# A routed expert network on one core: the first token list from 96 columns, the rest of the second list in a third piece, logits in groups of 24 matmuls, six search rounds

## The chip, the cores and the metric

The kernel runs on 1 core of one Trainium2 chip. The metric is the device time in microseconds (us) of one execution; several executions are made and the median is taken. The engines are TensorE (PE, its weight loads PEld), VectorE (DVE), ScalarE (ACT), GpSimd (POOL) and SyncE (SP), which here only issues DMA transfers.

## The reference

```python
# x (8, 3584, 192), weight (8 heads, 7 taps): a causal 7-tap filter, softmax weights per head
w = softmax(weight, axis=-1)
out = einsum('hk,bskhg->bshg', w, windows_of_7(x))      # -> 28672 tokens x 192
# routing: every (token, expert) pair in order of falling logit; a token goes to its first
# expert that still has room (3584 tokens each)
logits = out @ w_gate                                    # 28672 x 8
for idx in argsort(-logits.flatten()):
    tok, e = idx // 8, idx % 8
    if assigned[tok] < 0 and counts[e] < 3584: assigned[tok] = e; counts[e] += 1
# expert networks: h = relu(x @ w1[e]) (192 x 1024), y = h @ w2[e] (1024 x 192)
```

## The kernel before, in words

**Filter stage.** 16 half batches of 1792 tokens. `conv` (line 196) makes 8 PE matmuls per half batch, one per head (tile `cv`), ACT copies each to tile `a`, and the result is stored to `attn` in DRAM. DVE transposes `a` in four steps to `aT` (`transp`, 208); PE multiplies it with the gate matrix in six calls of four matmuls (`logits`, 217, tile `pl`; three `gate` steps of 8 matmuls each); `end` transposes the logits (tile `pt`) into `LT`, 16 columns per half batch, 256 in all, and takes each token's best logit (`top`).

**Routing in the background.** `Route` is a chain of generators whose steps `Steps.hook` (95) slips between the filter's and then the experts' instructions. A clock model (`Meter`, `Pace`) estimates when PE, DVE and ACT reach a point; a step is emitted only when its inputs should be there by that model. All engines run in program order, so a step emitted too early makes its engine wait. `thresh` finds a threshold `Ts`: tokens whose best logit is above it can be placed at once. From them two lists are made, each from 128 columns: `settle` marks them (`F`), `count` counts them with 8 matmuls, `place` computes each token's slot (18 matmuls with a base), `slots` prepares the operands, `sort` makes slot order with 128 one-hot matmuls (`oa`, eight per DVE instruction), `turn` transposes with 16 matmuls, `gather` adds up the list with 17 matmuls and `tokens` turns it into indices (`ia` where to write, `ja` where to read). The second list uses `sort4`, whose result goes through DRAM: two stores to `otab`, eight loads back (tile `X`, lines 546 and 563, all on SP); `gather` is emitted 10 us (`TURN`) after its last ACT copy by the model. `open` and `rounds` (743) then search the remaining tokens' thresholds in seven rounds (`ROUNDS`, 249), `final` marks the last tokens, and a last pair of lists (columns 128 to 255, then 0 to 127) is made with `sort4`.

**Experts.** 56 tiles of 512 tokens; tiles 0 to 7 come from the first list, 8 to 31 from the second, 32 to 55 from the last pair. Per tile 40 matmuls `ph` (`l1`, 1301) and 64 matmuls `y` of the tile before (`l2`, 1320), in eight steps f = 0 to 7. Rows are fetched two tiles ahead by four indirect DMAs on POOL (`gather`, 1268). Tiles 8 to 31 are transposed by DVE and a trip through DRAM (`scr`, lines 1396 to 1399, on SP); tile 0 by PE (`bg<-ident,xg`, `evac` to `xa` and `xd`). While tiles 0 to 7 run, the weights of the eight experts are loaded (`raw`), split into high and low parts (`wsplit`, 1219) and kept in DRAM (`kw`, `kv`), from which later tiles load them.

**Joints.** `half(0)`, `tail`, `half(1)` and `rest` run in this order (line 1535). `first` (1565) fetches tiles 0 and 1 as soon as `half(0)` is done (`got`). From half batch `LAG` = 13 on, the queue `left` of transposes and logit steps stands still until `got`, then two of its steps follow each `conv` matmul (`mid`, 1603). `idx_of` (1641) drains what is left of the second list before tile 8's rows are fetched (in tile 6), and of the last lists before tile 32's (in tile 30).

Of the kernel before, what the change touches and what calls it, by code (L numbers as in the profile page):

```python
# [248 lines left out]
ROUNDS = [(8, 1.0, False, 16)] + [(16, 1.0, False, 8)] * 2 + [(16, 0.5, True, 8)] * 2 + [(0, 0.0, True, 8)] * 2  # L249
# [10 lines left out]
class Route:  # L260
# [15 lines left out]
    def consts(self):  # L276
# [12 lines left out]
        self.g1 = cst.tile([128, 2], F32, name="g1")  # L289
        for h in range(2):  # L290
            P.tensor_scalar(self.g1[:, h:h + 1], pf, 1.0 + 128 * h, None, op0=OP.add)
# [81 lines left out]
    def settle(self, h):  # L373

        V, wk = self.nc.vector, self.wk
        s = slice(128 * h, 128 * h + 128)
        yield "cols", 128 * h + 128
        if h == 0:
            self.F = wk.tile([128, 8, G], BF, name="F")
        m = wk.tile([128, 128], F32, name="m_f")  # L380
        V.scalar_tensor_tensor(m, self.M1[:, s], self.Ts, self.M1[:, s], op0=OP.is_lt, op1=OP.add)
        for q in range(2):
            e = slice(4 * q, 4 * q + 4)
            V.tensor_tensor(self.F[:, e, s], self.LT[:, e, s], m[:, None, :].to_broadcast([128, 4, 128]),
                            op=OP.is_equal)
            yield PEW if q else None


    def count(self, F, h):
        nc, wk = self.nc, self.wk  # L390
        V, PE = nc.vector, nc.tensor
        s = slice(128 * h, 128 * h + 128)
        if h == 0:
            self.tot = [None, None]
            self.sl = wk.tile([128, G], F32, name="sl")
        ps = self.bg()
        for e in range(8):
            PE.matmul(ps[:, e:e + 1], F[:, e, s], self.ones[:, 0:1], start=True, stop=True, skip_group_check=True)
        t = self.tot[h] = wk.tile([128, 8], BF, name="tot%d" % h)
        nc.scalar.activation(t, ps[:, 0:8], AF.Copy)  # L400
        yield PEA

    def place(self, F, h, base):
# [3 lines left out]
        s = slice(128 * h, 128 * h + 128)  # L407
        SP = wk.tile([128, 8, 128], F32, name="X0")
        for q in range(2):
            ps = self.bg()  # L410
            f = F[:, 4 * q:4 * q + 4, s]
            PE.matmul(ps, self.U, f, start=True, stop=False, skip_group_check=True)
            for u in range(4):
                e = 4 * q + u
                o = ps[:, 128 * u:128 * u + 128]
                b = lambda t: t[:, e:e + 1].to_broadcast([128, 128])
# [3 lines left out]
            V.scalar_tensor_tensor(SP[:, 4 * q:4 * q + 4], ps.rearrange("p (e g) -> p e g", g=128), 1.0, f,  # L420
                                   op0=OP.add, op1=OP.mult)
            yield
        for u in range(2):
            z = slice(64 * u, 64 * u + 64)
# [3 lines left out]
    def columns(self, h, nt, base):  # L428
# [3 lines left out]
        ps = self.bg()  # L432
        PE.matmul(ps[:, 0:8], self.U, self.tot[h], start=True, stop=base is None)
        if base is not None:
            PE.matmul(ps[:, 0:8], self.ones, self.tot[base], start=False, stop=True)
        bi = wk.tile([128, 2, 8], I32, name="c_bi")
# [4 lines left out]
        c = wk.tile([128, 2, 8], F32, name="c_f")  # L441
        V.tensor_scalar(c[:, 0], bi[:, 0], 2.0, None, op0=OP.mult)
        V.tensor_scalar(c[:, 1], bi[:, 1], 2.0, 1.0, op0=OP.mult, op1=OP.add)
        oh = self.oh = wk.tile([128, 2, 8, 2, 16], BF, name="c_oh")
        V.tensor_tensor(oh[:, :, :, 0, 0:nt].rearrange("p w e t -> p (w e) t"),
                        self.iq[:, None, 0:nt].to_broadcast([128, 16, nt]),
                        c.rearrange("p w e -> p (w e)")[:, :, None].to_broadcast([128, 16, nt]), op=OP.is_equal)
        V.tensor_scalar(oh[:, :, :, 1, 0:nt].rearrange("p w e t -> p (w e) t"),
                        oh[:, :, :, 0, 0:nt].rearrange("p w e t -> p (w e) t"), self.g1[:, h:h + 1], None, op0=OP.mult)

    def slots(self, F, h, first):
# [4 lines left out]
        s = slice(128 * h, 128 * h + 128)  # L456
        si = wk.tile([128, 128], I32, name="m_i")
        qi = wk.tile([128, 128], I32, name="m_j")
# [3 lines left out]
        if first:  # L462
            V.tensor_copy(self.q, qi)
# [4 lines left out]
        for w in range(2):  # L468
            pw = wk.tile([128, 128], BF, name="pw")
            V.tensor_scalar(pw, si, 128.0 * w, self.p1, op0=OP.is_equal, op1=OP.mult)  # L470
            yield
            V.tensor_tensor(b[:, w], F[:, :, s], pw[:, None, :].to_broadcast([128, 8, 128]), op=OP.mult)
        yield

    def sort(self, h, nt, base, per=8):

        nc, wk = self.nc, self.wk
        V, A, PE = nc.vector, nc.scalar, nc.tensor
        O = self.O = wk.tile([128, 128, 16], BF, name="X1")
# [3 lines left out]
        while z < 128:  # L483

            t = max(q[0][1] + nc.las, free[0] if z % 32 == 0 else 0.0) if q else 0.0
            if q and t <= nc.pe:
                if z == 64:
                    yield from self.columns(h, nt, base)
# [11 lines left out]
            elif g0 < 128 and len(q) < 5:  # L500
# [13 lines left out]
    def sort4(self, h, nt, base):  # L514
# [10 lines left out]
        while z < 4:  # L525

            t = max(q[3][1] + nc.las, free) if len(q) > 3 else 0.0
            if len(q) > 3 and t <= nc.pe:
                if z == 2:
                    yield from self.columns(h, nt, base)  # L530
# [36 lines left out]
    def turn(self):  # L567
# [5 lines left out]
        for q in range(2):  # L573
            ps = self.bg().bitcast(BF)
            for j in range(8):
                PE.transpose(ps[:, 128 * j:128 * j + 128], self.O[:, :, 8 * q + j], self.identb)
            A.activation(OT[:, 8 * q:8 * q + 8].rearrange("p j q -> p (j q)"), ps, AF.Copy)
            yield PEA if q else None

    def gather(self, nt, first):  # L580
# [9 lines left out]
        for j in range(16):  # L590
            w, e = divmod(j, 8)
            PE.matmul(ps[:, 2 * nt * e:2 * nt * e + 2 * nt].rearrange("p (v t) -> p v t", t=nt), OT[:, j],
# [1113 lines left out]
```

## Time and profile before

| | |
|---|---|
| three executions | 1254.54, 1260.52, 1265.29 us, median 1260.52 |
| the profiled execution | 1251.99 us, its span 1250.2 us |
| busy share: PE, PEld, DVE, ACT, POOL | 97%, 83%, 78%, 44%, 43% |
| granted TensorE clock, mean | 0.994 |
| moved by DMA | 205.09 MB, 164 GB/s over the span |

The filter stage takes the first 161 us, the experts the rest. An idle time in a row's brackets is how long the engine stood still before it, and who released it. A matmul's duration includes its way through the pipeline, so costs are read from start to start. One matmul call with FP32 operands makes two rows of the trace.

### The profile page before, as it was taken

How to read it: one execution, taken by the hardware profiler on the slowest of the kernel's cores; microseconds unless marked ns; L12 is line 12 of the kernel's file. 1: busy time of each engine (PE TensorE's matmuls, PEld its weight loads, DVE VectorE, ACT ScalarE, POOL GpSimd, SP SyncE). 2: the span in 40 equal slices, each digit the busy share in tenths (PEclk: the TensorE clock that was granted, in tenths of full speed). 3: DMA queues.
4: the chain of work that ended last, by engine and by line, in shares of the span. 5: the costliest groups of instructions: out<-in, count | busy, mean ns of one | idle time of the engine just before them, and what ended most of it. 6: DMA issues, size and time to landing. Idle time of an engine off the chain costs nothing.

```text
span 1250.2 us, 21752 instructions
## 1 busy us (share of the span) xinstructions
PE 1208.1 (97%) x7702; PEld 1036.5 (83%) x7702; DVE 979.4 (78%) x2131; ACT 547.4 (44%) x1220; POOL 531.7 (43%) x528
## 2 busy tenths in 40 slices
PE   4999989999999999999999989999999999999997
PEld 2445568889988989889888879999999999999996
DVE  7388669889898898989888865777777777777772
ACT  4454555656444544444543333333443333443331
POOL 3000344535455545555454434445444544444522
PEclk9999999999999999999999999999999999999999
DMA  9999889999725463444344563114133222413100
GB/s 221 339 348 310 294 299 316 280 321 302 270 82 155 128 188 113 158 149 149 123 144 135 178 164 121 36 48 154 67 126 107 95 97 96 157 56 137 49 23 28
DMA packets 125188, 205.09 MB, mean 164 GB/s; under 512 B 21440, under 2 KB 85392, under 8 KB 121360
## 3 DMA queue, kind: packets, MB, share of 16 engines
q1 hardware_dynamic: 82464, 127.22, 31.9%
q0 software_dynamic: 21504, 44.07, 11.7%
q10 hardware_dynamic: 21104, 32.34, 7.8%
q8 instruction: 62, 1.02, 0.3%
q14 instruction: 54, 0.44, 0.1%
HBM read 118.64 MB, written 84.93 MB: 163 GB/s over the span
## 4 chain that ended last, share of the span: by engine, by line
PE 85%; DVE 6%; DMA 5%; issue 1%; SPq 1%; ACT 1%; POOL 1%; ACTq 0%; POOLq 0%; DVEq 0%
PE ph L56 40%; PE y L56 38%; PE bg L56 3%; PE cv L56 3%; DMA X<-in_x_dram 2%; DVE X L56 1%; DVE aT L56 1%; DMA wgr<-in_moe_w_gate_dram 1%; DMA raw<-in_moe_w_dram 1%; DMA X<-otab 1%; PE pl L56 1%; DMA xg<-attn,ja 1%; DVE hl L56 0%; PE px L56 0%; DMA otab<-X 0%
## 5 line engine op out<-in xcount | busy, mean ns | idle before, releaser
L56 PE MATMUL y<-w,hh 128*128 128x384 f32 x1792 | 536.8, 355 | 0.0
L56 ACT ACTIVATE hh<-ph 128x512 fp32r<-128x512 f32 x448 | 267.2, 597 | 486.3 <-PE ph L56 485.2
L56 PE MATMUL y<-w,hl 128*128 128x192 f32 x1792 | 449.7, 251 | 0.0
L56 DVE SCALAR_TENSOR_TENSOR hl<-ph,hh 128x512 fp32r<-128x512 f32 x448 | 308.5, 689 | 138.6 <-ACT hh L56 134.0
L56 PE MATMUL ph<-xa,w 128*128 128x512 f32 x1344 | 395.6, 402 | 0.0
L56 PEld LDWEIGHTS y<-w,hl 128*128 128x128 f32 x1792 | 341.7, 191 | 16.4
L56 PEld LDWEIGHTS y<-w,hh 128*128 128x128 f32 x1792 | 337.1, 188 | 20.4 <-issue 2.2
L56 PEld LDWEIGHTS ph<-xa,w 128*128 128x128 f32 x1344 | 218.9, 189 | 20.2 <-issue 1.0
L1348 POOL DMA_INDIRECT out_dram<-yo,ia x128 | 138.9, 1085 | 225.9 <-DVE yo L56 188.1
L1348 POOL DMA_INDIRECT out_dram<-yo,ib x96 | 95.9, 999 | 220.1 <-DVE yo L56 212.7
L56 PE MATMUL ph<-xd,w 128*128 128x512 f32 x448 | 178.9, 399 | 1.3 <-DVE xd L56 1.3
L56 PE MATMUL ph<-xd,dl 128*128 128x512 f32 x448 | 174.6, 390 | 0.2 <-DVE dl L56 0.2
L56 DVE STREAM_TRANSPOSE xs<-xg 32x128 f32<-32x128 f32 (+2 forms) x408 | 164.8, 404 | 6.6
L1273 POOL DMA_INDIRECT xg<-attn,ja x128 | 139.3, 1088 | 47.6 <-issue 40.4
L56 PE MATMUL cv<-X,TH 118*128 118x384 f32 x256 | 101.5, 523 | 19.5 <-DVE TH L56 12.5
L1273 POOL DMA_INDIRECT xg<-attn,jb x96 | 103.4, 1078 | 29.3 <-issue 29.3
L56 ACT ACTIVATE yt<-y 128x192 f32<-128x192 f32 x224 | 73.1, 326 | 94.3 <-PE y L56 92.3
L56 DVE TENSOR_TENSOR yo<-y,yt 128x192 f32<-128x192 f32 x224 | 79.5, 355 | 41.3 <-ACT yt L56 39.2
L56 PEld LDWEIGHTS ph<-xd,w 128*128 128x128 f32 x448 | 84.3, 188 | 21.4 <-DVE xd L56 1.7
L56 PEld LDWEIGHTS ph<-xd,dl 128*128 128x128 f32 x448 | 84.5, 189 | 19.7 <-issue 0.5
L56 PEld LDWEIGHTS cv<-X,TH 118*128 118x128 f32 x256 | 45.3, 198 | 49.9 <-issue 14.1
L56 ACT ACTIVATE a<-cv 128x384 f32<-128x384 f32 x128 | 59.5, 492 | 50.8 <-PE cv L56 33.0
(238 smaller groups left out, 893.1 us busy)
## 6 DMA issues: line engine op xcount, KB each, us to landing
attn<-a ACTq DMA_DIRECT2D x16, 1344.0 KB
w<-kw SPq DMA_DIRECT2D x14, 1536.0 KB
w<-kv SPq DMA_DIRECT2D x14, 1536.0 KB
kw<-w SPq DMA_DIRECT2D x48, 256.0 KB
kv<-w SPq DMA_DIRECT2D x32, 384.0 KB
X<-in_x_dram SPq DMA_DIRECT2D x17, 672.0 KB
X<-in_x_dram ACTq DMA_DIRECT2D x15, 672.0 KB
scr<-xs SPq DMA_DIRECT2D x96, 96.0 KB
```

The lines of the kernel that those rows point to most:

```text
L56: return f(*a, **k)
L1273: self.nc.gpsimd.indirect_dma_start(out=t[:, b], out_offset=None, in_=self.attn[0:rows], in_offset=bass.IndirectOffsetOnAxis(ap=idx[b], ax ...
L1348: st = self.nc.gpsimd.indirect_dma_start(out=self.out, out_offset=bass.IndirectOffsetOnAxis(ap=idx, axis=0), in_=o, in_offset=None, bounds ...
```

## The change

The lists are made from three pieces of columns instead of two halves (`PARTS`): the first list from 0 to 95 with `sort` of 96 columns; the second from 96 to 223 with `sort4` as before, and, added up into the same list, 224 to 255 with `sort` and `turn` of 32 columns. The third piece's marking, count and totals (`third`) stand between the second's `sort4` and its `gather`, where `open` stood; `open` opens `rest`. The last lists keep the halves. One of the two rounds (16, 1.0, False, 8) is left out. From half batch 13 on, the 24 logit matmuls of a half batch are one step ahead of the transposes.

```diff
+PARTS = ((0, 96), (96, 128), (224, 32))
+HALVES = ((0, 128), (128, 128))
-ROUNDS = [(8, 1.0, False, 16)] + [(16, 1.0, False, 8)] * 2 + [(16, 0.5, True, 8)] * 2 + [(0, 0.0, True, 8)] * 2
+ROUNDS = [(8, 1.0, False, 16)] + [(16, 1.0, False, 8)] + [(16, 0.5, True, 8)] * 2 + [(0, 0.0, True, 8)] * 2
...
-    def place(self, F, h, base):
+    def place(self, F, part, bases):
...
-                if base is not None:
-                    PE.matmul(o, b(self.tot[base]), self.ones, start=False, stop=False, skip_group_check=True)
-                PE.matmul(o, b(self.tot[h]), self.U, start=False, stop=(u == 3), skip_group_check=True)
+                for p in bases:
+                    m = p[1]
+                    PE.matmul(o, self.tot[p][:, e:e + 1].to_broadcast([m, 128]), self.ones[0:m, 0:n],
+                              start=False, stop=False, skip_group_check=True)
+                PE.matmul(o, self.tot[part][:, e:e + 1].to_broadcast([n, 128]), self.U[0:n, 0:n],
+                          start=False, stop=(u == 3), skip_group_check=True)
...
-        while z < 128:
+        while z < n:
...
-                if z == 64:
-                    yield from self.columns(h, nt, base)
+                if z == n // 64 * 32:
+                    yield from self.columns(part, nt, bases)
...
-        def half(h):
-            if h == 0:
-                yield from r.thresh(0.905)
-            yield from r.settle(h)
-            yield from r.count(r.F, h)
-            if h:
-                yield from r.counts(NE)
-            yield from r.lists(r.F, TA, h, 0 if h else None, *((ia, ja) if h else (ia0, ja0, 8, 4)),
-                               between=r.open() if h else None, swap=h == 1)
+        def early():
+            yield from r.thresh(0.905)
+            yield from r.settle(PARTS[0])
+            yield from r.count(r.F, PARTS[0])
+            yield from r.listed(r.F, TA, PARTS[0], ())
+            yield from r.tokens(TA, ia0, ja0, 8, 4)
+
+        def second():
+            yield from r.settle(PARTS[1])
+            yield from r.count(r.F, PARTS[1])
+            yield from r.listed(r.F, TA, PARTS[1], PARTS[0:1], between=third())
+            yield from r.listed(r.F, TA, PARTS[2], PARTS[0:2])
+            yield from r.tokens(TA, ia, ja, swap=True)
+
+        def third():
+            yield from r.settle(PARTS[2])
+            yield from r.count(r.F, PARTS[2])
+            yield from r.counts(NE)
 
         def rest():
+            yield from r.open()
             yield from r.rounds()
...
-        bg = Steps(nc, r, (half(0), tail(), half(1), rest()))
+        bg = Steps(nc, r, (early(), tail(), second(), rest()))
...
+        def gates(i):
+            for u in range(3):
+                gate(i, u)
...
                 if i and h == 0:
+                    if i >= LAG:
+                        left.append(partial(gates, i - 2))
                     for u in range(4):
                         left.append(partial(k.transp, i - 1, u))
-                        if i > 1:
+                        if 1 < i and (u == 3 or i < LAG):
                             left.append(partial(gate, i - 2, u) if u < 3 else partial(end, i - 2))
```

How the instructions move is shown at three places.

**PE, after the first list's last matmul.** The row `bg<-c_oh,X` is the last of the list's `gather`. Before, with 15 `conv` matmuls still to come:

```order
L56 MATMUL bg<-c_oh,X_1471 128x32
L56 MATMUL cv<-X,TH 128x384 x4
L56 MATMUL pl<-aT,c_mu 32x128 x8
L56 MATMUL cv<-X,TH 128x384
L56 MATMUL pl<-aT,c_mu 32x128 x8
L56 MATMUL cv<-X,TH 128x384
```

Now, with 21 still to come, down to the transposes of tile 0's rows (`bg<-ident,xg`):

```order
L56 MATMUL bg<-c_oh,X_1398 128x32
L56 MATMUL cv<-X,TH 128x384 x4
L56 MATMUL pl<-aT,c_mu 32x128 x24
L56 MATMUL cv<-X,TH 128x384 x2
L56 MATMUL pt<-ident,L 128x128
L56 MATMUL cv<-X,TH 128x384
L56 MATMUL pl<-aT,c_mu 32x128 x24
L56 MATMUL cv<-X,TH 128x384 x2
L56 MATMUL pt<-ident,L 128x128
L56 MATMUL cv<-X,TH 128x384 x5
L56 MATMUL pl<-aT,c_mu 32x128 x24
L56 MATMUL cv<-X,TH 128x384 x2
```

The list comes six `conv` matmuls earlier, and each half batch's logits stand in one block.

**PE, after the second list's gather** (in tile 4). Before, the experts' matmuls follow at once:

```order
L56 MATMUL bg<-c_oh,X_2968 128x32
L56 MATMUL ph<-xa,w_2889 128x512 x3
L56 MATMUL ph<-xd,w_2889 128x512
L56 MATMUL ph<-xd,dl 128x512
L56 MATMUL y<-w_2672,hh 128x384
```

Now the third piece's `place` follows, 26 matmuls of which this is the start:

```order
L56 MATMUL bg<-c_oh,X_2847 128x32
L56 LDWEIGHTS U
L56 MATMUL bg<-F,U 128x128
L56 LDWEIGHTS tot_1017
L56 MATMUL bg<-ones,tot_1017 128x32
L56 LDWEIGHTS tot_2109
L56 MATMUL bg<-ones,tot_2109 128x32
L56 LDWEIGHTS tot_2887
L56 MATMUL bg<-U,tot_2887 128x32
```

Its `sort`, `turn` and `gather` come later in tile 4.

**SP, around the last pair of lists** (`otab_82` is the second store, the row after it the loads back). Before, the last list, in tiles 28 and 29:

```order
L546 DMA otab_81<-X_9012 128x2048
L1396 DMA scr_99<-xs 32x6x128 x4
L1398 DMA xs<-scr_99 128x512
L1399 DMA xs<-scr_99 64x512
L546 DMA otab_82<-X_9013 128x2048
L563 DMA X_9383<-otab_81 16x16x128 x4
```

Now, the first of the pair, in tiles 25 and 26:

```order
L1409 DMA scr_100<-xs 32x6x128 x4
L1411 DMA xs<-scr_100 128x512
L1412 DMA xs<-scr_100 64x512
L1244 DMA w_8565<-kw_83 128x3072
L1245 DMA dl<-kd_91 64x1024
L557 DMA otab_82<-X_8228 128x2048
L574 DMA X_8620<-otab_81 16x16x128 x4
```

and the last list, in tile 27:

```order
L557 DMA otab_81<-X_8770 128x2048
L1251 DMA w_8964<-kv_101 128x3072
L557 DMA otab_82<-X_8771 128x2048
L574 DMA X_9133<-otab_81 16x16x128 x4
```

The last list's second store no longer stands behind the `scr` trip; the first one's stands behind a weight load.

More of the change, by code (lines that the diff above doesn't have):

```diff
@@ L430, in columns @@
         nc, wk = self.nc, self.wk
         V, PE = nc.vector, nc.tensor
[L432 to L436, printed above, removed]
+        c0, n = part
+        ps = self.bg()[0:n]
+        PE.matmul(ps[:, 0:8], self.U[0:n, 0:n], self.tot[part], start=True, stop=not bases)
+        for p in bases:
+            PE.matmul(ps[:, 0:8], self.ones[0:p[1], 0:n], self.tot[p], start=False, stop=p == bases[-1])
```

155 lines of the change are left out of this document (82 added, 73 removed).

## The prediction

> **What bounds the kernel now.** First the page's busy shares, then busy time by stretch, then what PE waited for.
>
> ```profile
> PE 1208.1 (97%) x7702; PEld 1036.5 (83%) x7702; DVE 979.4 (78%) x2131; ACT 547.4 (44%) x1220; POOL 531.7 (43%) x528
> 300.00:400.00 100.00, 99.39 (x568) 89.46 (x568) 88.81 (x203) 49.05 (x123) 53.96 (x48) 1.00 0.56 178
> 700.00:750.00 50.00, 46.42 (x383) 40.56 (x382) 36.19 (x73) 19.22 (x38) 19.59 (x18) 0.95 0.55 148
> ```
>
> The columns of a stretch are its length, busy PE, PEld, DVE, ACT, POOL, the granted clock, the DMA share and GB/s. PE has work almost throughout: 42 us of the 1250 are idle. So a matmul added or removed costs what it takes on PE, work of other engines costs nothing unless PE waits for it, and what can be won is in the idle times. The waits of PE over the span:
>
> ```profile
> PE bg L56 <- DMA X<-otab: 3.3, 1, 3.3
> PE bg L56 <- DVE F L56: 1.7, 2, 1.3
> ```
>
> and those from 100 to 165 us, around the filter's end:
>
> ```profile
> PE pl L56 <- DVE aT L56: 1.6, 3, 0.8
> PE bg L56 <- DMA xg<-attn,ja: 1.5, 1, 1.5
> PE ph L56 <- DVE xd L56: 1.3, 1, 1.3
> ```
>
> The numbers are the sum, the times and the longest. Each lies at a place that the change touches. (The other large ones come in the first 50 us, where nothing is changed.)
>
> **Part 1, the filter's end: -5.4 us.** The timeline of PE:
>
> ```profile
> 132.11 2.07 PE L56 MATMUL bg<-X,oa 128*128 128x16 bf16 x32
> 134.03 2.18 PE L56 MATMUL cv<-X,TH 118*128 118x384 f32 x6
> 136.05 1.16 PE L56 MATMUL bg<-identb,X 128*128 128x128 bf16 x16
> 137.04 2.15 PE L56 MATMUL cv<-X,TH 118*128 118x384 f32 x6
> 139.15 0.55 PE L56 MATMUL bg<-c_oh,X 128*128 128x32 bf16 x16
> 139.55 2.83 PE L56 MATMUL cv<-X,TH 118*128 118x384 f32 x8
> 142.31 0.64 PE L56 MATMUL pl<-aT,c_mu 128*32 128x128 f32 x16
> 142.88 0.91 PE L56 MATMUL cv<-X,TH 118*128 118x384 f32 x2
> 143.72 0.64 PE L56 MATMUL pl<-aT,c_mu 128*32 128x128 f32 x16
> 158.46 0.33 PE L56 MATMUL bg<-ident,xg 128*128 128x128 f32 x1 [1.53 <-DMA xg<-attn,ja]
> 163.41 0.51 PE L56 MATMUL ph<-xd,w 128*128 128x512 f32 x1 [1.31 <-DVE xd L56]
> ```
>
> Three things go away. The first list's `sort` loses 32 of its 128 matmuls, 132.11 to 134.03: 1.9 us. A `conv` call costs 0.69 us in a run (139.55 to 142.31 for four) and 0.84 us between two logit steps (142.88 to 143.72); with one logit block per half batch instead of three, six such returns fall away, 0.15 us each: 0.9 us. And the waits: the list is done six `conv` calls earlier, so tile 0's rows land earlier against PE: 1.5 us for `xg`, 1.3 us for `xd` (its transposes now stand two `conv` calls ahead of the first `ph`, before right before it), 0.8 us of the `aT` waits. Together 6.4 us.
>
> Two come in their place. What matters is from the list's last matmul to the rows' landing:
>
> ```profile
> 141.71 1.26 DVE L56 TENSOR_SCALAR m_i<-m_f,off 128x32 int32<-128x32 f32 x1
> 145.25 0.18 DVE L56 TENSOR_SCALAR ja<-m_y 128x32 int32<-128x32 f32 x1
> 145.35 3.55 DVE L56 STREAM_TRANSPOSE aT<-a 128x768 f32<-128x768 f32 x4
> 150.51 1.00 POOL L1273 DMA_INDIRECT xg<-attn,ja  x1 [0.31 <-issue]
> ```
>
> From 139.55 the indices took until 145.4, the fourth fetch was issued at 150.5 and had landed at 158.5: 18.9 us, of which some 2 us are the index operations of 1.2 us like the one at 141.71, which run beside a weight split on POOL; that split now stands behind the fetches. So 16.8 to 18.9 us. In the change the second logit block needs four DVE transposes (3.6 us) behind the indices (3.8 us from the list, without the 2): 7.4, against seven `conv` calls and a block, 6.7 us of PE work; a wait of 0.7 us (0 to 2). Up to where it needs the rows PE has 16 `conv` calls (11.0), three logit blocks of 1.7 with their returns (5.6), transposes (0.4) and that wait, 17.7 us: a wait of up to 1.2 us, of which I take 0.3, as the splits are moved. Sum 6.4 - 1.0 = 5.4; bounds 2.5, if the waits only change their names, and 6.4.
>
> **Part 2, the third piece on PE: +5.9 us.** It adds its count, `place`, `columns`, `sort`, `turn` and `gather`. The price of `place` comes from the second list's:
>
> ```profile
> 196.73 0.22 PE L56 MATMUL bg<-ones,tot 128*128 128x128 bf16 x1
> 197.78 0.22 PE L56 MATMUL bg<-U,tot 128*128 128x128 bf16 x1
> ```
>
> From the first to the last of sixteen such starts is 1.05 us, 0.22 of it for a 512-wide row between them: 0.055 us each, 26 matmuls 1.4 us. `sort` of 32 columns is the 32-matmul block above, 1.9; `turn` is 136.05 to 137.04, 1.0; `gather` 0.5; count, totals and columns 0.5. Six insertions among the experts' matmuls break PE's overlap, 0.1 us each by the returns above: 0.6. Sum 5.9 (5 to 7.5). The second list's own 128 columns cost what they did. All this is on PE's path. On DVE and ACT it lies beside PE's work; if that cover were gone, PE would wait, which is part 5.
>
> **Part 3, a round less: -1.0 us.** One round on PE:
>
> ```profile
> 488.95 0.31 PE L56 MATMUL bg<-r_c,onesf 128*128 128x8 f32 x2
> 497.55 0.23 PE L56 MATMUL bg<-r_cc,ones 128*128 128x120 bf16 x1
> 507.06 0.17 PE L56 MATMUL bg<-ones,r_c 128*8 128x1 bf16 x1
> ```
>
> Six matmuls in four places; the six rows sum to some 1.3 us, but a good part of a row is the pipeline's end. I take 0.1 us each and 0.1 for each of four insertions (0.6 to 1.3). The round's DVE work costs nothing: PE is busy 99.4% of the stretch from 300 to 400, so nothing waits for it there. Its effect is on when the last lists come: the last list's `gather` moves from tile 29 to tile 28.
>
> **Part 4, the second list's way through DRAM: -0.7 us.**
>
> ```profile
> 239.36 1.22 PE L56 MATMUL bg<-oa,X 128*32 128x128 bf16 x32
> 253.71 0.55 PE L56 MATMUL bg<-c_oh,X 128*128 128x32 bf16 x16 [1.64 <-DMA raw<-in_moe_w_dram]
> ```
>
> PE waits 1.6 us for the list's data (`X<-otab`; the row names the DMA that ended last). From the start of the last `sort4` block it had 12.7 us of work ahead of the `gather`; in the new order there are some 13.4 (the third piece's count and totals stand between). Bounds -1.6 (gone) and +1.5 (that DMA stretch is busy, and tiles start earlier).
>
> **Part 5, new small waits: +1.2 us.** The third piece's steps are emitted by the clock model. Of the second list's six groups one waited, 1.3 us for `F`. Seven new groups at that rate: 1.5; I take 1.2, since one of them, the `columns`, hides behind `sort` (0 to 3).
>
> **Part 6, the last two lists: -4.3 us.**
>
> ```profile
> 667.50 0.60 SPq L1231 DMA_DIRECT2D w<-kw  x1
> 668.00:675.00 7.00, 7.00 (x42) 6.37 (x41) 6.83 (x14) 3.51 (x8) 2.47 (x2) 1.00 0.93 322
> 696.63 1.19 PE L56 MATMUL bg<-oa,X 128*32 128x128 bf16 x32
> 698.51 0.32 SPq L546 DMA_DIRECT2D otab<-X  x1
> 708.38 0.55 PE L56 MATMUL bg<-c_oh,X 128*128 128x24 bf16 x16 [0.26 <-issue]
> 730.21 1.19 PE L56 MATMUL bg<-oa,X 128*32 128x128 bf16 x32
> 736.00 0.59 SPq L546 DMA_DIRECT2D otab<-X  x1
> 746.00 0.58 PE L56 MATMUL bg<-c_oh,X 128*128 128x24 bf16 x16 [3.32 <-DMA X<-otab]
> 746.42 0.77 PE L56 MATMUL ph<-xd,w 128*128 128x512 f32 x1
> 751.60 0.34 PE L56 MATMUL y<-w,hh 128*128 128x384 f32 x1
> ```
>
> Without a queue in front, the data is there 11.7 us after the last `sort4` block starts (696.63 to 708.38). For the last list the store left SP only at 736.00, behind the `scr` trip, 5.8 us after its block's start instead of 1.8: PE waited 3.3 us, and the five `ph` and eight `y` matmuls from 746.42 to 751.60 took 5.2 us instead of some 2.8, at a granted clock of 0.95 in that stretch: 2.4 us more. With the 0.3 of the first of the two, 5.9 us. In the new order the last list's store stands behind nothing that waits, and PE reaches its `gather` four steps of 2.29 us (13 calls each, at 568 calls per 100 us in the stretch above), 0.7 and its own 1.2 after the block starts, 11.1 us: a wait of 0.6. The first list of the pair has 11.7 us of cover, but its store is issued just after a weight load like that at 667.50, whose traffic fills the DMA engines until 675: I take 1.0 us. Neither should cost clock: the waits of 1.3 to 1.6 us did not. So 5.9 - 1.6 = 4.3; bounds 5.9 gained and 2 lost.
>
> **Sum.** -5.4 + 5.9 - 1.0 - 0.7 + 1.2 - 4.3 = -4.3 us. The profiled execution, 1252.0, would become 1247.7. The median of the runs shown is 8.5 us above it, so the forecast for a median is 1260.5 - 4.3 = 1256 us, 0.3% less, which a measurement of this kernel, good to about 1%, does not tell from no change.
>
> **Rivals.** *More is won*: every wait of parts 1, 4 and 6 goes and none comes: -6.4 + 5.0 - 1.3 - 1.6 - 5.9 = -10.2, 1250 us. For it: the runs are slower than the profile, so their waits may be longer. Against it: covers of 11 us for 11.7 needed.
>
> *Slower: the last pair's store is caught behind the weight load.* The load is 1.5 MB with 0.25 beside it, 7 us at a share of 0.93. If SP issues it less than about 4 us ahead of the store, PE waits up to 6 us instead of 1.0 and loses 2.4 us of clock: +7.2, sum +2.9, 1263 us. For it: load and store are neighbours on SP. Against it: the load needs only a buffer that the tile before has left, so SP, free of the `scr` trip some 4 us before the store, can send it that early. The Trainium skill, "DMA: Bandwidth & Descriptors", section "Queues, rings and completion order", says that descriptors of one issuing engine are taken in ring order on each DMA engine. By that rule the store could not pass the load; no row here shows the two side by side. On the clock, "TensorE: Matmul & The Clock Gate" there, Part 1, has it halve after an idle window of about 3.4 us; the trace agrees with 3.32 us and the slow rows behind it, and by that rule a wait of 5 us would cost clock too.
>
> *Slower: the third piece's steps come too early*, as DVE is 89% busy: if all seven groups wait 1.3 us, 9.1 instead of 1.2, sum +3.6, 1264 us. Against it: only one in six did.
>
> *The early list does not help*: the rows' landing takes 18.9 us or more again, part 1 falls to 2.5, sum -1.4, 1259 us. For it: POOL issues the same eight fetches in a row.
>
> **Chances.** The forecast 0.42, more won 0.20, caught store 0.15, early steps 0.10, no help 0.13. The likeliest case's own bounds are 1251 to 1261. The range takes in the rivals and the runs' own spread of 5 us to either side: 1247 to 1265, with 2 in 10 outside. Faster by over 1% is below 1248: a part of the second case, 0.13. Slower by over 1% is above 1273, two bad cases at once: 0.06. Within 1%: 0.81.
>
> **What would show it.** The `xg` and `xd` waits gone and the first `ph<-xd` near 158 us instead of 163.4; one `aT` wait under 2 us; 32 extra one-hot matmuls in tile 4 with few waits; the rows `bg<-c_oh` of the last lists with waits near 1 us and a granted clock of 1.00 from 680 to 750. The forecast is wrong if the first `ph<-xd` stays near 163, if the third piece brings waits of more than 3 us, or if the pair's first `gather` waits 3 us or more.

## The result and the profile after

The changed kernel takes 1271.14 us (median of 12 runs) against 1257.95 for the kernel before on the same chip: a ratio of 1.0093, 95% interval 1.0074 to 1.0112, some 12 us slower. Forecast were 1256 us and a range to 1265. The change was measured twice more on other chips: 1.0057 (1.0038 to 1.0076) and 1.0048 (1.0031 to 1.0065). The profiled execution took 1263.32 us with a span of 1261.3 (before 1251.99 and 1250.2). From its page:

```profile
PE 1215.5 (96%) x7766; PEld 1043.1 (83%) x7766; DVE 954.5 (76%) x2091; ACT 543.0 (43%) x1207; POOL 532.9 (42%) x530
```

PE has 7 us more work, and stands still 4 us longer. Where, the timeline of PE says, with each idle time in its row's brackets:

```profile
162.15 0.46 PE L56 MATMUL bg<-ident,L 128*128 128x128 f32 x1 [2.36 <-ACT L L56]
172.01 0.96 PE L56 MATMUL ph<-xa,w 128*128 128x512 f32 x3 [0.44 <-DVE hl L56]
174.20 0.96 PE L56 MATMUL ph<-xa,w 128*128 128x512 f32 x3 [0.77 <-DVE hl L56]
245.29 0.55 PE L56 MATMUL bg<-c_oh,X 128*128 128x32 bf16 x16 [1.19 <-DMA kw<-w]
...
489.01 0.22 PE L56 MATMUL bg<-ident,r_v 8*128 8x8 f32 x1 [1.50 <-DVE r_v L56]
531.13 0.26 PE L56 MATMUL bg<-r_cc,ones 128*128 128x120 bf16 x1 [2.97 <-DVE r_cc L56]
...
701.73 0.55 PE L56 MATMUL bg<-c_oh,X 128*128 128x24 bf16 x16 [1.89 <-DMA X<-otab]
```

The waits for `xg` and `xd` (1.5 and 1.3 us) and the last list's 3.3 us are gone. New are a wait for `L` (the copy of a logit block) and two for `hl` (the low part of the experts' hidden layer, whose high part is `hh`) in tile 0, waits in the search rounds (489, 531 and one of 1.24 us at 588), where before had one of 0.6 us, and one for the first list of the last pair (701.73). The half clock of this profile comes behind the waits of 2.36, 1.19 and 2.97 us. The starts of the tiles (each tile's first `ph<-xa` row), with two of the experiments below, show where the time goes:

| tile starts, us | 0 | 1 | 4 | 5 | 16 | 24 | 31 |
|---|---|---|---|---|---|---|---|
| before | 161.2 | 177.1 | 244.5 | 266.1 | 473.5 | 624.7 | 775.6 |
| the change, first profile | 153.6 | 174.2 | 242.6 | 272.2 | 479.7 | 639.4 | 787.1 |
| the change, repeated (c1) | 152.2 | 172.8 | 241.2 | 271.1 | 476.8 | 628.2 | 774.7 |
| without the pieces (e4) | 156.6 | 173.5 | 240.9 | 262.2 | 470.5 | 622.8 | 764.3 |
| stores put off (e17) | 153.5 | 168.1 | 240.7 | 270.4 | 476.1 | 627.5 | 774.9 |

In the first profile 7.6 us are won up to tile 0 (some 3 of them in the first 60 us, where nothing is changed), 1.9 are left at tile 4; tile 4 costs 8 us more, tiles 16 to 23 another 8.5, and the end of the lists gives 3 back.

### The profile page after: what moved, and what is told of

Same layout as the page of the kernel before. It is cut to its first block, busy times and chain, and to the rows that moved or that the text cites. A ratio compares the mean times of both kernels' runs of the same rounds, so it can differ in the third digit from the quotient of the medians.

```text
span 1261.3 us, 21823 instructions
## 1 busy us (share of the span) xinstructions
PE 1215.5 (96%) x7766; PEld 1043.1 (83%) x7766; DVE 954.5 (76%) x2091; ACT 543.0 (43%) x1207; POOL 532.9 (42%) x530
## 4 chain that ended last, share of the span: by engine, by line
PE 87%; DMA 5%; DVE 5%; issue 1%; ACT 1%; SPq 1%; POOL 0%; another core or an unknown queue 0%; ACTq 0%; POOLq 0%; DVEq 0%
PE ph L56 40%; PE y L56 38%; PE bg L56 3%; PE cv L56 3%; DMA X<-in_x_dram 1%; PE pl L56 1%; DMA raw<-in_moe_w_dram 1%; DVE X L56 1%; DVE aT L56 1%; DMA wgr<-in_moe_w_gate_dram 1%; DMA otab<-X 1%; ACT hh L56 0%; DVE hl L56 0%; PE px L56 0%; DMA kw<-w 0%
## 5 line engine op out<-in xcount | busy, mean ns | idle before, releaser
L56 DVE SCALAR_TENSOR_TENSOR hl<-ph,hh 128x512 fp32r<-128x512 f32 x448 | 307.8, 688 | 161.2 <-ACT hh L56 135.2
```

The lines of the kernel that those rows point to most:

```text
L56: return f(*a, **k)
```

## The experiments

Every ratio is to the kernel before, measured beside it on the same chip.

**The rounds alone, the pieces alone.** Four kernels take the change apart.

```diff
 e1: the kernel before, with
+ROUNDS = [(8, 1.0, False, 16)] + [(16, 1.0, False, 8)] + [(16, 0.5, True, 8)] * 2 + [(0, 0.0, True, 8)] * 2
 e2: the changed kernel, with
+ROUNDS = [(8, 1.0, False, 16)] + [(16, 1.0, False, 8)] * 2 + [(16, 0.5, True, 8)] * 2 + [(0, 0.0, True, 8)] * 2
 e5: as e2, and the logits in steps of 8 matmuls as before
 e4: the kernel before, with six rounds and the logits in groups of 24
```

> The kernel before with six search rounds, nothing else changed. In the change the tiles that hold the rounds (16 to 24) lost 8.5 us, with PE waits on r_v (3.2 us in all) and r_cc (3.9 us, one of 2.97 us with a halved clock behind it). Theory A, the round left out does it: the last rounds, which end in a chain of small DVE operations between two PE transposes (r_v), now stand at other places of the tiles, where DVE is not free in time; then this kernel shows such waits too and takes 1258 + 6 = 1264 us (4 to 9 us more than before). Rival B, the third piece does it, by moving all rounds back by most of a tile: this kernel shows no r_v waits over 0.5 us in sum and takes 1258 - 1 - 3 = 1254 us (a round less, and the last lists earlier as in the change).

> The changed kernel with seven rounds again. Theory A, the round left out brings the waits: tiles 8 to 25 take what they took before, +1 us for the round more, and the time is some 1271 - 8 + 1 = 1264 us. Rival B, the third piece's shift brings them: the first three rounds stand at the same places as in the change (tiles 9, 12 and 15), waits on r_v and r_cc stay at 5 us or more in sum, and the time stays at 1271 us or above, the more as the last lists come a tile later.

> The kernel before with the three pieces of columns only: seven rounds, logit steps of 8 matmuls. If the grouping of the logits brings what tile 0 lost (20.6 us instead of 16.0, with waits on L and hl), tile 0 lasts about 16 us here and tile 1 starts some 4 us earlier than in the kernel before, start-up apart; then the time is 2 to 4 us below that of the changed kernel with seven rounds. If the early list itself brings it (tail of logits against the experts' first steps), tile 0 lasts 20 us here too, and the two agree within 1 us. In both cases the third piece costs 6 to 8 us in tile 4.

> The change without its three pieces: two halves, six rounds, logits in groups of 24. Theory D, the pieces are what costs and the other two parts are gains of their own: the six rounds alone gave 0.57% (7 us), the grouping saved some 4 us beside the pieces (1.0141 to 1.0118 with seven rounds, and 5 us to the start of tile 1), so this takes about 1 - 0.0057 - 0.003 = 0.991 of before, 11 us less. Rival E, the grouping only pays where the list comes early: nothing beyond the six rounds, 0.994.

| | rounds | logits by 24 | pieces | ratio | 95% interval |
|---|---|---|---|---|---|
| e1 | six | | | 0.9943 | 0.9923 to 0.9964 |
| e4 | six | yes | | 0.9938 | 0.9920 to 0.9956 |
| e5 | seven | | yes | 1.0141 | 1.0120 to 1.0162 |
| e2 | seven | yes | yes | 1.0118 | 1.0098 to 1.0139 |
| the change (c1) | six | yes | yes | 1.0057 | 1.0038 to 1.0076 |

Theories A and B both fall: the round left out is a gain of some 7 us, alone (e1) and beside the pieces (e2 against c1, on two chips), and neither e1 nor e2 shows waits on `r_v` and `r_cc` beyond the one of 0.6 us that before has. Theory D holds for the pieces, which cost 1.2% (e4 against the change on one chip), and rival E for the logits, which bring nothing clear of the error without the early list and perhaps 3 us with it (e5 to e2, intervals that overlap). e5's own question gets neither answer: its tile 0 lasts 17.6 us, and the kernel takes 4 us more than e2, not less. The gain of the rounds lies where the prediction looked for it. In e1 PE reaches both `gather` blocks of the last lists without a wait:

```profile
659.98 0.55 PE L56 MATMUL bg<-c_oh,X 128*128 128x24 bf16 x16
692.97 0.55 PE L56 MATMUL bg<-c_oh,X 128*128 128x24 bf16 x16
```

From tile 5 to tile 31 e1 takes 502.0 us, before 509.5. With the pieces and seven rounds (e2) the last list comes so late that it is drained for tile 32's rows with no work left to put between, and PE stands still; the round left out spares this wait:

```profile
766.53 0.58 PE L56 MATMUL bg<-c_oh,X 128*128 128x24 bf16 x16 [11.23 <-DMA X<-otab]
```

**Do the waits in the rounds belong to the change?** c1 is the change itself again; e6 emits the steps later.

```diff
 e6: the changed kernel, with
-        nc.lat, nc.las = (0.8, 1.2)
+        nc.lat, nc.las = (1.6, 2.4)
```

> The changed kernel as it is, once more, beside the other two. The kernel with seven rounds has the same instructions on PE, DVE and ACT up to 480 us, and lost nothing in tiles 9 to 15, where the profile of the change showed waits on r_c and r_cc and copies hh that started 2 to 3 us after their matmuls instead of 0.4. Theory C, those late starts belonged to that execution or that chip: here they are gone, tiles 9 to 24 take 282 to 284 us instead of 292, and the ratio to before is 1.002 to 1.004 instead of 1.009. Rival A, the order of the instructions brings them: they come again at the same places, and the ratio is 1.009 again.

> The changed kernel with the clock model's two reserves in the expert stage doubled (0.8 to 1.6 us for DVE, 1.2 to 2.4 for ACT), so that background steps are emitted later. Theory A1, the steps come too early for where DVE stands: the waits on r_v, r_cc, r_c and F fall from 9 us in sum to under 3 and no half clock follows one; 1271 - 8 = 1263 us. Rival A2, DVE is held up by other engines' work by amounts that no small reserve covers (an operation of 0.4 us took 2.05 us beside POOL's work): the waits stay above 6 us, at other places, and the time is within 3 us of 1271.

c1: 1.0057, and theory C holds for the waits: tiles 9 to 23 take 282.2 us (first profile 292.3), with no wait over 0.2 us in the rounds. The ratio is above the 1.002 to 1.004 that went with it. e6 came to 1.0036 (1.0022 to 1.0050); as c1 has no such waits to cure, it says nothing on A1 and A2, and its last list waited 4.3 us. What differed shows at one place where the first profile and e2 have the same instructions and PE runs alike. The first profile, PE and then ACT, whose copy `hh` comes from the `ph` that ends with that row:

```profile
369.28 0.39 PE L56 MATMUL ph<-xd,dl 128*128 128x512 f32 x1
...
372.31 0.60 ACT L56 ACTIVATE hh<-ph 128x512 fp32r<-128x512 f32 x1 [4.30 <-PE ph L56]
```

and e2:

```profile
369.26 0.39 PE L56 MATMUL ph<-xd,dl 128*128 128x512 f32 x1
...
369.69 0.60 ACT L56 ACTIVATE hh<-ph 128x512 fp32r<-128x512 f32 x1 [1.69 <-PE ph L56]
```

In the first profile ACT, free and with its matmuls done, starts 2.6 us late; DVE's `hl` behind it is late, and a search step that was to find DVE free makes PE wait. Copies `hh` from 340 to 640 us that start more than 1.2 us after both the end of their matmuls and ACT's instruction before: 8 in the first profile, none in all fifteen kernels run on chips where before takes 1248 to 1250 us, 6 to 11 in the three run on a chip where it takes 1258.9 (e14 to e16 below). The first result's chip, with 1257.95, is like the latter, but the profile of before, taken there, has none. So the late copies go with the chip, its state or the single execution, and not with the order of the instructions; what delays them stays open.

**Tile 0.** The change starts it early and loses it again. From here on c1 is the profile of the change. PE, then ACT with its DMA issue (ACTq), then two stretches:

```profile
159.13 0.33 PE L56 MATMUL bg<-ident,L 128*128 128x128 f32 x1 [1.08 <-ACT L L56]
170.55 1.65 PE L56 MATMUL ph<-xa,w 128*128 128x512 f32 x3 [3.46 <-DVE hl L56]
```

```profile
157.39 0.31 ACTq L205 DMA_DIRECT2D attn<-a  x1
157.75 0.60 ACT L56 ACTIVATE hh<-ph 128x512 fp32r<-128x512 f32 x1 [4.59 <-PE px L56]
...
168.77 0.52 ACT L56 ACTIVATE w<-raw 128x384 fp32r<-128x384 f32 x1 [4.90 <-DMA raw<-in_moe_w_dram]
```

```profile
160.00:165.00 5.00, 5.00 (x55) 3.83 (x52) 3.87 (x8) 2.79 (x8) 0.00 (x0) 1.00 1.03 322
170.00:175.00 5.00, 4.43 (x10) 2.82 (x11) 4.33 (x8) 2.71 (x5) 0.00 (x0) 0.50 0.98 375
```

ACT waits twice: behind the issue of the last `attn` store, so `hh` and `L` come 4 us late; and for a weight piece (`raw`). By the trace's semaphores the store's issue was released at 157.34 by an earlier transfer that shares its semaphore, a `raw` load that SP had issued at 153.14: both waits are for weights. DMA is full (share 1.03), and with the 3.46 us wait the granted clock is halved. Four kernels try the possible causes.

```diff
 e8:  -TAIL = (2, 3, 4, 7, 8, 9, 12, 13)
      +TAIL = (2, 3, 4, 10, 11, 12, 18, 19)
 e10: wsplit: self.wload() ahead of the piece's S.dma_start(self.kept...), not behind
 e14: -        A.dma_start(attn[i * 1792:(i + 1) * 1792]...
      +        (P if i == NHB - 1 else A).dma_start(attn[i * 1792:(i + 1) * 1792]...
 e17: the kept stores of the first 8 pieces collected, issued on SP in at(1)
```

> The changed kernel with the last two half batches' logit steps set further apart in tile 0 (calls 2, 3, 4, 10, 11, 12, 18, 19 instead of 2, 3, 4, 7, 8, 9, 12, 13). In the change PE waited 1.0 to 2.4 us in tile 0 for ACT's copy L of the logits just made, and then 1.2 to 3 us for DVE's hl. Theory F, the steps follow too closely: the wait for L goes, tile 0 is 1 to 2 us shorter, the time 1 to 2 us less than the change's. Rival G, DVE and ACT are behind there by all the work of the filter's end, and the wait only moves to hl or to the next step: tiles 0 and 1 together stay within 0.7 us of the change's.

> The changed kernel with each weight piece's next load put ahead of the stores of the piece just split, on SP. In the repeated run of the change PE waited 1.08 us for L and 3.46 us for hl in tile 0, the second behind ACT's weight copy at 168.77, which had waited 4.90 us for a load (raw) that SP issued at 157.65; DMA was busy at shares of 0.88 to 1.03 from 150 to 165 us. Theory H, the weights' way through a full DMA is what bounds tile 0 now: the load goes out some 1.5 us earlier and ahead of 0.5 MB of stores, the wait for hl falls below 1 us, tile 0 takes 17 to 18 us instead of 20.7, the time 3 us less, a ratio of 1.003 to before. Rival I, tile 0 is held by the pile of work on DVE and ACT: hl stays above 2.5 us, the ratio at 1.0057.

> The changed kernel with the last half batch's attn store issued by POOL instead of ACT. In the repeated run of the change ACT's first hh of tile 0 started at 157.75, 4 us after its matmuls (ended by 153.8), directly behind the issue of that store at 157.39, whose data was there at 153.2: the issue waits for an earlier transfer, in a stretch with DMA shares of 0.88 to 0.97, and all of ACT's work stands behind it. Theory N, that wait in ACT's queue is what tile 0 loses: hh starts within 1 us of its matmuls, the waits for L and hl (1.1 and 3.5 us) are under 1 us in sum, tile 0 takes 16 to 17.5 us instead of 20.7, the ratio to before falls by 0.003 to about 1.002. Rival O, the weights' loads in the same full stretch come too late whoever issues the store: hh is early, but hl still waits 2 us or more behind ACT's weight copies, and the time moves by less than 1.5 us.

> The changed kernel with the stores of the first expert's split weights (3.3 MB, which nothing reads before tile 29) put off to the start of tile 1; nothing else changed. Theory P, tile 0 waits for DMA: from 140 to 165 us the DMA engines run at shares of 0.74 to 1.03, and 3.3 MB at some 300 KB per us are 11 us of that. Then the weight pieces land in time, the last attn store goes out early, the waits for L and hl in tile 0 (4.5 us in the repeated run) fall below 1.5 us, tile 0 takes 17 to 18 us instead of 20.7, and the ratio falls by 0.002 to 0.003 against the change on the same chip, unless the put-off stores make tile 1 or 2 wait. Rival Q, tile 0 is held by the number of operations on ACT and DVE: the waits stay above 3 us.

e8, 1.0045 (1.0030 to 1.0061): rival G, the wait for `L` goes and comes back behind `hl`:

```profile
173.00 0.80 PE L56 MATMUL ph<-xa,w 128*128 128x512 f32 x1 [5.48 <-DVE hl L56]
```

e10, 1.0059 (1.0034 to 1.0083): tile 0 takes 19.1 us instead of 20.7, with waits of 1.9 and 2.1 us left, and tile 8 takes 20.9 against 18.3, which nothing here ties to the order of the loads: nothing won, and neither theory cleanly right. e14, 1.0091 (1.0067 to 1.0115) on the chip of late copies (the first result, on a chip like it, was 1.0093): `hh` is early and the wait for `L` gone, but the weights are late all the same and PE waits 1.96 us at 173.58, rival O:

```profile
158.19 0.60 ACT L56 ACTIVATE hh<-ph 128x512 fp32r<-128x512 f32 x1 [0.66 <-PE ph L56]
...
171.79 0.52 ACT L56 ACTIVATE w<-raw 128x384 fp32r<-128x384 f32 x1 [3.09 <-DMA raw<-in_moe_w_dram]
```

e17, 1.0027 (1.0015 to 1.0038) beside c2's 1.0048 on that chip (the intervals overlap), shows theory P and its limit. With 3.3 MB of stores out of the way tile 0 takes 14.6 us and waits for nothing over 0.3. But tile 1 and 2 take 4.6 us longer than in the change beside it, the wait for the weights comes at the start of tile 2, and at tile 4 hardly anything is left (240.7 against c1's 241.2 and c2's 242.1). PE, and DMA there:

```profile
193.51 0.73 PE L56 MATMUL ph<-xa,w 128*128 128x512 f32 x2 [3.67 <-DVE hl L56]
```

```profile
155.00:160.00 5.00, 5.00 (x79) 3.46 (x78) 5.00 (x8) 2.84 (x7) 3.93 (x5) 1.00 1.00 335
185.00:190.00 5.00, 4.84 (x28) 4.19 (x27) 0.41 (x3) 0.00 (x0) 0.00 (x0) 1.00 1.01 359
```

So tiles 0 to 3 wait on DMA: what goes earlier at one place comes later at the next. The first 200 us of before, of c1 and of e17 say the same (the last two columns are the DMA share and GB/s):

```profile
0.00:200.00 200.00, 172.22 (x1421) 104.38 (x1422) 142.58 (x317) 99.85 (x245) 43.11 (x77) 0.99 0.99 306
0.00:200.00 200.00, 174.98 (x1410) 109.71 (x1410) 140.46 (x313) 100.51 (x249) 44.03 (x79) 0.97 0.98 307
0.00:200.00 200.00, 174.53 (x1412) 109.75 (x1413) 141.93 (x316) 101.83 (x249) 46.18 (x80) 0.98 0.98 306
```

All three have moved the same 61 MB by then, with the DMA engines at 0.98 or more, whenever tile 0 starts.

**The third piece and the lists' way through DRAM.** PE in tile 4 of c1, the piece's first and last `place` row, and the stretch behind them:

```profile
243.97 0.55 PE L56 MATMUL bg<-c_oh,X 128*128 128x32 bf16 x16 [1.34 <-DMA kw<-w]
244.38 0.22 PE L56 MATMUL bg<-F,U 128*128 128x128 bf16 x1
...
246.48 0.18 PE L56 MATMUL bg<-U,tot 32*128 32x32 bf16 x1
```

```profile
248.00:250.00 2.00, 2.00 (x6) 1.41 (x6) 1.83 (x8) 0.00 (x0) 0.00 (x0) 0.50 1.05 387
```

In e4 the same `gather` waits as long, the experts' matmuls follow at once, and the clock stays:

```profile
249.87 0.55 PE L56 MATMUL bg<-c_oh,X 128*128 128x32 bf16 x16 [1.32 <-DMA raw<-in_moe_w_dram]
...
250.00:252.00 2.00, 2.00 (x25) 1.79 (x23) 1.51 (x5) 0.74 (x2) 0.00 (x0) 1.00 1.07 395
252.00:254.00 2.00, 2.00 (x13) 1.70 (x12) 1.97 (x8) 1.05 (x4) 0.00 (x0) 1.00 1.05 408
```

For the first list of the last pair, c1's SP and the DMA shares behind it:

```profile
674.15 0.58 SPq L1244 DMA_DIRECT2D w<-kw  x1
...
676.71 0.32 SPq L557 DMA_DIRECT2D otab<-X  x1
677.07 9.46 SPq L574 DMA_DIRECT2D X<-otab  x8
```

```profile
675.00:680.00 5.00, 4.79 (x64) 4.16 (x61) 3.55 (x6) 1.88 (x5) 0.00 (x0) 1.00 1.05 323
680.00:685.00 5.00, 5.00 (x31) 4.58 (x30) 4.83 (x10) 2.59 (x6) 2.46 (x2) 1.00 0.97 247
```

The weight load goes out 2.6 us ahead of the store, and PE waits:

```profile
689.33 0.55 PE L56 MATMUL bg<-c_oh,X 128*128 128x24 bf16 x16 [2.87 <-DMA X<-otab]
```

```diff
 e11: -TURN = 10.0
      +TURN = 14.0
 e12: -                    S.dma_start(self.otab[z // 2 - 1], O[z // 2 - 1])
      +                    A.dma_start(self.otab[z // 2 - 1], O[z // 2 - 1])
```

> The changed kernel with 14 us instead of 10 us set for a list's way through DRAM, so that PE reaches each gather with 4 us more of experts' matmuls done. In the repeated run PE waited 1.34 us for the second list and 2.87 us for the first of the last pair, whose store was issued at 676.71, 2.6 us behind a weight load of 1.5 MB on the same queue, with DMA shares of 1.05 and 0.97 until 685. Theory J, PE only comes too early: both waits go, tile 26 takes 24.4 us instead of 27.4, the time 4 us less, a ratio of 1.0025. Rival K, the wait was cover for other late work, or the gather now comes so late that the list itself is late: PE waits elsewhere, 1.0057.

> The changed kernel with the two stores of a list (otab) issued by ACT, on a queue without weight loads; the eight loads back stay on SP. Theory L, the store stands in line behind the weight load only because they share a queue: it passes, the wait of 2.87 us for the first list of the last pair falls below 1 us. Rival M, the weight load fills the DMA engines whatever queue a transfer is on (shares of 1.05 and 0.97 until 685), or the loads back wait behind it on SP all the same: the wait stays above 2 us. In time no more than 1 to 3 us, near the resolution; the wait decides.

e11, 1.0015 (0.9999 to 1.0031), is level with before: theory J. PE comes later and finds the data:

```profile
693.79 0.55 PE L56 MATMUL bg<-c_oh,X 128*128 128x24 bf16 x16
...
732.62 0.55 PE L56 MATMUL bg<-c_oh,X 128*128 128x24 bf16 x16 [0.22 <-issue]
```

and tile 26 takes 23.1 us instead of 27.4. The profiles alone do not show the gain, though: e11 starts tile 31 at 775.4 us, c1 at 774.7, since the moved steps cost elsewhere. It is in the other executions, whose clock comes up below. e12, 1.0042 (1.0029 to 1.0056), is the change within the error: rival M. The wait is 3.58 us, longer, with the store on a queue of its own. The trace tells which of M's two reasons it is. SP's last four loads back wait for the store to land, 7.8 us here and 4.8 in c1; the first row is e12's wait on SP, the others all that the DMA queues move from 679.9 to 684 us, right behind the store's issue on ACT at 679.85 (packets, MB, share):

```profile
SPq L574 <- DMA otab<-X: 7.8, 1, 7.8
q1 hardware_dynamic: 108, 1.16, 99.8%
q0 software_dynamic: 8, 0.00, 0.3%
```

That is SP's queue (q1) and 8 small packets of POOL's; the first packet of ACT's (q10) starts at 684.29. So it is the store that is late, whatever queue it is on, and not the loads back: PE's `gather` starts 4.4 us after they begin to go out, in c1 4.6. The other runs agree. Where the weight load goes out 2.4 to 4.6 us ahead of the store, these loads follow the store's issue after 7.2 to 9.0 us (8.9 in e12); where 7 us or more lie between, after 3.2 to 5.4.

**Together.** e13 and e16 are e4 with e10's order, and with e14's store and a `TURN` of 12; e15 and e18 are the change with `TURN` 14 and e14's or e17's edit; c2 and e4 again stand beside e17 and e18.

> The change without its pieces (two halves, six rounds, logits in groups of 24), with the load-first order of the weights. If theory H holds for this kernel too, its waits for xd and hl in tile 0 (1.18 and 0.87 us) get shorter: 0.992 of before, 2 us less than without (0.9938). If the early list alone makes the weights late, no change: 0.994.

> The changed kernel with the last attn store on POOL and 14 us for the lists' way through DRAM. The second alone gave 1.0015. If the two causes are apart from each other and theory N holds, 1.0015 - 0.003 = 0.9985, 2 us less than before; under rival O 1.001. In both cases the third piece's 8.6 us in tile 4 and the early list's 6 us are left against each other, and it stays behind the version without pieces (0.994).

> The version without pieces (two halves, six rounds, logits in groups of 24) with the last attn store on POOL and 12 us for the lists' way through DRAM. There ACT stood idle for 1.6 us ahead of its first hh, PE waited 1.2 us for xd, 0.9 for hl and 1.3 for the second list's data. If these waits go: 0.9938 - 0.002 = 0.992. If they only change their names, 0.994.

> The changed kernel as it is. On a chip where the kernel before takes 1248 to 1250 us: ratio 1.0057 as in the repeated run, no waits on r_v or r_cc over 0.6 us. On a chip where it takes 1258 us: 1.009, and some 8 us of such waits.

> The version without pieces (two halves, six rounds, logits in groups of 24) once more, beside the change: 0.994 on a chip of the first kind, up to 0.998 on one of the second.

> The changed kernel with the put-off stores and 14 us for the lists' way through DRAM. The second alone took 0.0042 off the ratio. If theory P holds both add up: 0.006 to 0.007 below the change, level with before (0.999 to 1.000), and what is left of the pieces' cost is the third piece in tile 4. Under Q: 0.004 below the change.

e13 0.9958 (0.9943 to 0.9974), e15 1.0036 (1.0018 to 1.0054), e16 0.9978 (0.9959 to 0.9997), c2 1.0048, e4 again 0.9929 (0.9914 to 0.9944), e18 1.0019 (1.0004 to 1.0035). No cure makes the change faster than before, and none adds to e4. e15 and e16 ran where copies come late, so they are not set against the others: e15 against e14 there is again `TURN`, 0.0055. e18 is no better than e11: the two cures do not add up. None of the four combinations (e13, e15, e16, e18) came as low as its first theory had it (0.992, 0.9985, 0.992 and 0.999). e4, six rounds and the grouped logits without the pieces, takes 1240 to 1242 us where before takes 1248 to 1250 and the change 1256: the best version, and e1 is within its error.

## Why the prediction was wrong, point by point

**Part 1, forecast -5.4, measured -1.0.** The step itself was right. Five profiles without the early list (three of them with the logits grouped) start tile 0 at 156.6 to 161.2, mean 158.7; eleven with early list and grouping, on the same kind of chip and the first, at 151.7 to 154.4, mean 153.3: -5.4, with no more than 0.3 us of it from the first four half batches. But the sum stopped there. Tile 4 starts at 242.9 without (mean of the five) and 241.9 with (c1, c2, e2, e8, e10, e12 and the first profile). The step that failed is "Three things go away ... Together 6.4 us": the part counted what goes up to the first `ph`, took that as kept to the end, and asked of no transfer that follows whether it can come earlier too. The DMA share of 0.99 over before's first 200 us would have raised the question; e17, and the same 61 MB moved by 200 us in all three kernels, show that DMA is the bound there.

**Part 2 and 4, forecast +5.9 and -0.7, measured +8.3** (tile 4 takes 29.9 us in c1, 21.6 before). On PE the piece costs 2.2 us for `place` (forecast 1.4), 0.2 for `columns`, 2.0, 1.1 and 0.7 for `sort`, `turn` and `gather`, 6.3 in all. "0.6 for six insertions" was the mis-sized term, beside `place`: the experts' matmuls of tile 4 take 2.3 us more (21.6, before 19.3), with some 3.4 us at half clock behind the `gather`'s wait and `place`. The sum had no clock term for tile 4. In c2 the half clock lasts 6.8 us there and the tile 31.5. The wait of part 4 stayed at 1.2 to 1.8 us.

**Parts 3, 5 and 6, forecast -1.0 + 1.2 - 4.3 = -4.1, measured -5.9** (tile 5 to 31: c1 503.6, before 509.5). The last list's 3.3 us and their clock went, as forecast; the third piece's steps brought no waits of their own. The first of the pair waits 1.9 to 2.9 us, where 1.0 was taken: the rival of the caught store, with the load 2.6 us ahead of the store in c1 as its condition had it (4.4 in the first profile), though at a quarter of its price or less: 0.9 to 1.9 us more than taken instead of the 7.2 (by its own terms, 5.0 and 2.4, it should be 7.4), and in the three profiles of the change a clock that stayed at 1.00. That was luck: in e8, e10, e12, e14 and e17 the same wait, 2.2 to 3.8 us, has some 3.4 us at half clock behind it, so "Neither should cost clock" does not hold either. The rival's reason, the ring order, is not borne out: e12's store had a queue without the load, and was as late. "Queues, rings and completion order" in the Trainium skill's "DMA: Bandwidth & Descriptors" has descriptors taken in order within one ring; e12's store shared none with the load, so these runs neither show nor refute the rule.

**The sum.** -1.0 + 8.3 - 5.9 = +1.4 us by the profiles, forecast -4.3 (c1's own starts tile 31 0.9 us ahead of before's, which was 1.6 us later than the mean at tile 4). The medians differ by 7.6 and 6.6 us. The profiled executions of the change were the shortest of theirs (1250.70 of 1250.70 to 1256.49, 1252.50 of 1252.50 to 1258.91). Its runs have a mean granted clock of 0.990 on both chips, those of before 0.996 and 0.994, those of e4 0.997 and 0.996. The profiled executions of the change have 0.993 and 0.992, the others of theirs 0.989 and 0.990 in the mean. An estimate from this: 0.002 to 0.004 less clock is 5 to 9 us more at half speed, so 2.5 to 4.7 us lost, near the 4.9 and 4.0 us by which the medians lie above the profiles. e4 and c1, on one chip, give the same picture: c1's profile starts tile 31 10.4 us later, 8.6 of them from tile 4, and the medians differ by 15.2. The waits of the last pair's first list, which e8 and four others show with a half clock behind them, are a likely place; but the rows of the slower executions are not there, so this stays an estimate. The prediction had a clock term in one place only, where it vanishes.

**The result itself, 1.0093,** holds some 5 us more than the other two chips show; its profile has the late copies and 8.5 us lost in the rounds. No rival had that.

**The rivals.** "The early list does not help" came nearest in kind, with a bound of 2.5 us for what is left of part 1, and the wrong reason, the fetches on POOL. "Steps too early" did not happen: from tile 1 to tile 8 c1 has no wait over 0.4 us but that of the `gather` in tile 4. The list of signs was met nearly point by point, `xg` and `xd` gone, the first `ph<-xd` earlier, few waits in the third piece, no half clock from 680 to 750 in the three profiles, and the kernel is slower: the signs asked whether each gain comes, none whether it lasts.

## What to carry to other kernels

A gain is worth what is left of it at the next point where everything must be there. Before a stage is started earlier, look at the DMA share of the stretch around it: here, at 0.98 over the first 200 us, the earlier start was handed back within four tiles. And take a change apart before timing the whole: here six rounds gain 7 us and the pieces lose 15, and the whole shows only the 7 us between them.

## What was not expected of the hardware

A wait of 1.3 us with 2.2 us of small matmuls (26 in `place`, of 32 and 128 columns) behind it is followed by some 3.4 us at half clock, the same wait with the experts' 512-column matmuls behind it by none. In e11 a wait of 0.70 us between the two halves of `place` has 6.8 us behind it:

```profile
247.95 0.22 PE L56 MATMUL bg<-F,U 128*128 128x128 bf16 x1 [0.70 <-DVE asm L56]
...
250.00:252.00 2.00, 2.00 (x7) 1.61 (x6) 1.83 (x9) 0.29 (x1) 0.00 (x0) 0.50 1.04 370
```

Length alone does not decide it: in e15 the same block with a wait of 0.63 us has none behind it, and in e6 the block, with no wait over 0.2 us but with two of the experts' matmuls between its halves, has 3.4 us. Nor are small matmuls needed: in e13 a wait of 2.37 us with the experts' matmuls right behind has 3.4 us too. Part 1 of "TensorE: Matmul & The Clock Gate" in the Trainium skill speaks of idle windows of about 3.4 us. The waits of 2.37 us (e13) and 2.23 us (e17, the last pair's first list) are shorter and have the half clock all the same, one of 2.87 us in c1 has none, so here the length of the wait is not the whole rule. In c1 and e11 wait and small matmuls together are about 3.4 us long, as if such matmuls hardly counted as work; that was not tried by itself.

One DMA issue on ACT held up four microseconds of ACT's computing (157.39): ACT stood still until a transfer of another queue had landed, and e14, with that store on POOL, has its `hh` 0.66 us after ACT's last work. And one DVE operation of 0.4 us took 2 us beside POOL's work in the first profile (`r_cc`, 2.05 us at 529.02); that POOL is the cause is not shown.
